# Grouping the products of probabilities and values of a sink attention by whole query tiles

## The chip, the cores and the metric

The kernel runs on one core of one Trainium2 chip. The metric is the time of one execution on the device in microseconds (us), the median over several runs. The core has TensorE (PE in the profile, with its weight loads listed apart as PEld), VectorE (DVE), ScalarE (ACT), GpSimd (POOL) and SyncE (SP, which issues most transfers).

## The reference

Three layers follow each other, all in f32, with 2 batches of 768 positions. The first is an attention of 8 heads of 64 with a sliding window and sink positions; the change is in it.

```
scores = q @ k.T / 8                                   # per head, 768 x 768
keep   = (pos_k < n_sink) | (0 <= pos_q - pos_k < window)   # n_sink 4, window 128
a      = softmax(where(keep, scores, -1e9))
x      = concat_heads(a @ v)                           # 2 x 768 x 512
```

The second layer is `h = relu(x @ w_in)` (512 to 1024), a convolution over 3 neighbouring positions, `h * sigmoid(conv)` and `@ w_out` (1024 to 512). The third is an attention of four experts with a causal mask, of which each position takes the best two. The weights of the second layer come as 64-bit floats.

## The kernel before

The first layer works on query tiles of 128 positions. A batch has 6 tiles, and a tile has 4 pairs of heads, so a batch has 24 steps: step 4q + p is pair p of query tile q. All the work of a layer is laid out on one axis of steps by `run_phases`: every stage of the work on a pair or a tile has a lag in steps, and at each step the stages run in the order that the string `ORD1` gives. What is emitted first stands first in its engine's queue, and each engine works through its queue in order. Batch 1 starts at step 24 and the second layer at step 30.

For batch 0 the stages that matter are these, with the method, the line by which the profile knows it, and the step at which it runs:

- S, scores (`a1_S`): TensorE multiplies queries by keys of the pair's two heads (L484), at the pair's own step. VectorE adds the mask and takes the row maximum (L486), ScalarE takes the exponential with the row sum (L489). Both are emitted with S. Batch 1 does its scores with smaller multiplications (L471).
- T, transposes (`a1_T`): TensorE transposes the probabilities (L545) one step later, and ScalarE copies them to SBUF (L501, tile `PT`).
- V, values (`a1_V`): TensorE multiplies values by the transposed probabilities (L587) into one PSUM bank that holds the output of the whole query tile (`a1O`). It is taken at a tile's first V and read by `x_norm` at step 4q + 10. The lag of V is `pv`, and the third element of its entry says how many steps are gathered: a group is run as a whole, at the lag counted from its first member.
- r, rT, rB: the reciprocals of the sums (L497) at step 4q + 4, their transpose on TensorE (L514) at 4q + 5, and two transfers to DRAM and back that spread them over partitions (R).
- sT, sL, sV (from the third tile on): the probabilities of the sink positions are transposed (L567) at 4q + 6, split (L574) and multiplied by the sinks' values (L595) into the same bank at 4q + 8.
- xm, xh, xl: the output is scaled by the reciprocals (L529), and split in two parts for the next layer (L501, L617).

Between these, background work turns the 64-bit weights of the second layer into f32: ScalarE takes absolute values (L339), VectorE shifts and merges bits (L343, L346, L349, L413). It is emitted by a credit that each step tops up, so its places in the queues do not depend on V.

The order at one step, of batch 0 alone, is: S, sL, V, rB, sV, xm, rT, sT, T, r, xh. The lines that decide where V runs are these:

```
first = i - i % g[0] if g else i
at.setdefault(o + math.floor(lag + first * rate), []).append((k, m, i, fn))
```

Before, V of pairs 0 and 1 of tile q runs at step 4q + 4, and V of pairs 2 and 3 at step 4q + 6.

Of the kernel before, what the change touches and what calls it, by code (L numbers as in the profile page):

```python
# [70 lines left out]
BG0 = 550  # L71
BG1 = 650
BG2 = 1200
LAGS = ((1, 2, 1, 4, 3, 4, 5, 5, 2, 7, 7, 9, 11), (1, 1, 2, 6, 3, 4, 5, 3, 2, 5, 6, 7, 7))
LAGM = (1, 2, 3)
A2_N = 2
EVT = 'aaadadada'
# [11 lines left out]
class Kernel:  # L89
# [538 lines left out]
    def attn_phase(self, b, start, lags, misc):  # L628

        r, gather, tr, pv, sT, sL, sV, rB, rT, xm, xh, xl, halo = lags  # L630
        steps = [(qt, pr) for qt in range(NT) for pr in range(NPAIR)]

        def each(fn):
            return lambda i: fn(b, *steps[i])

        def last(fn, lo=0):
            def go(i):
                qt, pr = steps[i]
                if pr == NPAIR - 1 and qt >= lo:
                    fn(b, qt)  # L640

            return go

        st = {
            "r": (r, last(self.a1_r)), "rT": (rT, last(self.a1_rT)), "rB": (rB, last(self.a1_rB)),
            "xm": (xm, last(self.x_norm)), "S": (0, each(self.a1_S)), "T": (tr, each(self.a1_T)),
            "V": (pv, each(self.a1_V), 4 if b else 2), "gather": (gather, each(self.a1_gather)), "sT": (sT, last(self.a1_sinkT, 2)),
            "sL": (sL, last(self.a1_sinkL, 2)), "sV": (sV, last(self.a1_sinkV, 2)), "xh": (xh, last(self.x_hi)),
            "xl": (xl, last(self.x_lo)), "halo": (halo, last(self.x_halo)), "misc": (0, misc[0]), "more": (0, misc[1])}
        return lambda names: (start, len(steps), [st[n] for n in names.split()], RATE1 if b else 1)  # L650
# [466 lines left out]
    def program(self, general):  # L1117
# [5 lines left out]
        with ExitStack() as ctx:  # L1123
# [34 lines left out]
            else:  # L1158
# [18 lines left out]
                self.fixed()  # L1177
                first = [self.attn_phase(b, b * NSTEP, LAGS[b], self.attn_misc(b)) for b in range(B)]
                m1 = NSTEP + MLP_START
# [109 lines left out]
```

## Time and profile before

| | |
|---|---|
| median of 3 runs | 371.52 us (371.45 to 371.52) |
| profiled execution, its time | 371.99 us |
| its span, first to last instruction | 370.1 us |
| around the span | 1.89 us |
| mean granted TensorE clock | 0.996 |

The profile is of one execution. The busy time of an engine is the union of its instructions' spans. Matmuls overlap, and their ends are modelled, so that PE's busy share is not its share of peak. f32 matmuls stand as two records each in the trace, so 16 records of L587 are the 8 products of two pairs of heads. In the chain of waits, a piece lasts until the next piece of the chain can begin, so its times are what one operation adds to the chain. In the timeline, brackets give the idle time of an engine before an instruction, and what ended it.

### The profile page before, as it was taken

Reading aid. Unit: us, or ns where it says so; the run is one execution under the profiler, and the core shown is the slowest. Engines: PE = TensorE matmul, PEld = TensorE weight load, DVE = VectorE, ACT = ScalarE, POOL = GpSimd, SP = SyncE. Lnnn points to the kernel's source line nnn. Section 1 sums busy time; section 2 is a strip of 40 time slices with the busy share of each in tenths; the row PEclk is TensorE's granted clock in tenths of the full one; section 3 lists DMA queues with packets and bytes.
Section 4 is the critical chain, followed back from the end, with each engine's and each line's share of the span. In section 5 each row is a group of like instructions: output and inputs, shape, how many; then the busy total and the mean of one; then the engine's idle time right before and its main releaser. Section 6 shows DMA issues by size and latency. Waiting matters only on the chain.

```text
span 370.1 us, 8877 instructions
## 1 busy us (share of the span) xinstructions
PE 359.7 (97%) x3166; PEld 331.7 (90%) x3166; DVE 273.1 (74%) x850; ACT 261.2 (71%) x746; POOL 118.8 (32%) x230
## 2 busy tenths in 40 slices
PE   8999999899999999999999999999999999999994
PEld 5687877899899999999999999999999899978983
DVE  5689899999887997878756766238668688578731
ACT  4999998766886766546746766249878687849841
POOL 7014120444432342844421322500034144406310
PEclk9999999999999999999999999999999999999998
DMA  7943865353342311000211010000000010101112
GB/s 178 362 140 126 241 220 173 116 186 129 103 128 69 105 30 31 6 25 25 63 44 45 1 58 3 0 2 0 2 3 1 17 42 22 40 0 58 58 51 75
DMA packets 20404, 27.53 MB, mean 74 GB/s; under 512 B 2080, under 2 KB 12928, under 8 KB 20352
## 3 DMA queue, kind: packets, MB, share of 16 engines
q1 hardware_dynamic: 19120, 26.22, 22.2%
q10 hardware_dynamic: 1232, 0.66, 0.9%
q8 instruction: 27, 0.44, 0.5%
q14 instruction: 25, 0.20, 0.2%
HBM read 23.68 MB, written 3.19 MB: 73 GB/s over the span
## 4 chain that ended last, share of the span: by engine, by line
PE 77%; DVE 12%; ACT 5%; issue 2%; POOL 2%; DMA 1%; SPq 0%; ACTq 0%; DVEq 0%
PE psB L797 15%; PE psB L753 14%; PE psB L947 9%; PE psB L1061 5%; PE psB L1037 5%; PE psB L875 5%; PE psB L1085 4%; PE psB L587 4%; PE psB L484 4%; PE psB L545 3%; DVE P L486 3%; PE psB L1008 3%; PE psB L1007 3%; PE psB L471 2%; ACT P L489 2%
## 5 line engine op out<-in xcount | busy, mean ns | idle before, releaser
L797 PE MATMUL psB<-g,wouthf 128*128 128x256 f32 x384 | 70.5, 281 | 0.2 <-POOL g L782 0.2
L797 PEld LDWEIGHTS psB<-g,wouthf 128*128 128x128 f32 x384 | 58.9, 188 | 0.6 <-POOL g L782 0.4
L753 PE MATMUL psB<-xh,winhf 128*128 128x258 f32 x192 | 56.5, 294 | 0.0
L1025 POOL TENSOR_SCALAR P<-P,r 128x256 f32<-128x256 f32 (+5 forms) x48 | 30.3, 644 | 79.4 <-DVE r L1023 32.6
L753 PE MATMUL psB<-xh,winlf 128*128 128x258 f32 x192 | 54.3, 283 | 0.0
L753 PE MATMUL psB<-xl,winhf 128*128 128x258 f32 x192 | 54.2, 282 | 0.0
L797 PE MATMUL psB<-g,woutlf 128*128 128x256 f32 x192 | 53.8, 280 | 0.0
L489 ACT ACTIVATE P<-P,nm 128x260 f32<-128x260 f32 (+2 forms) x96 | 46.5, 486 | 10.1 <-DVE nm L486 9.9
L782 POOL TENSOR_TENSOR g<-ht,g 128x256 fp32r<-128x256 f32 x48 | 33.2, 691 | 52.4 <-ACT g L776 46.9
L1014 ACT ACTIVATE P<-P,nm 128x256 f32<-128x256 f32 (+5 forms) x48 | 32.1, 669 | 13.5 <-DVE nm L1013 7.8
L769 ACT ACTIVATE ht<-ht 128x256 f32<-128x256 f32 x48 | 20.1, 418 | 28.3 <-DVE ht L767 28.2
L774 DVE SCALAR_TENSOR_TENSOR ht<-ht 128x256 f32<-128x256 f32 x48 | 24.2, 505 | 18.8 <-ACT ht L769 18.8
L753 PEld LDWEIGHTS psB<-xh,winhf 128*128 128x128 f32 x192 | 36.4, 189 | 0.3 <-ACT ht L756 0.2
L753 PEld LDWEIGHTS psB<-xl,winhf 128*128 128x128 f32 x192 | 36.5, 190 | 0.0
L753 PEld LDWEIGHTS psB<-xh,winlf 128*128 128x128 f32 x192 | 36.2, 189 | 0.0
L797 PEld LDWEIGHTS psB<-g,woutlf 128*128 128x128 f32 x192 | 36.2, 189 | 0.0
L1010 DVE CUSTOM_DVE_ANT_0 P<-psB,causal 128x384 f32<-128x384 f32 (+3 forms) x64 | 30.3, 503 | 5.7 <-PE psB L1008 5.2
L760 POOL TENSOR_SCALAR ht<-ht,cw 128x256 f32<-128x256 f32 x24 | 15.1, 627 | 59.8 <-ACT ht L756 52.3
L767 DVE SCALAR_TENSOR_TENSOR ht<-ht,cw 128x256 f32<-128x256 f32 x48 | 28.3, 589 | 1.7
L545 PE MATMUL psB<-ident,P 128*128 128x128 f32 x176 | 29.0, 281 | 0.2
L947 PE MATMUL psB<-yh,wqh 128*128 128x256 f32 x96 | 27.2, 283 | 0.0
L947 PE MATMUL psB<-yl,wqh 128*128 128x256 f32 x96 | 27.0, 281 | 0.0
(172 smaller groups left out, 961.3 us busy)
## 6 DMA issues: line engine op xcount, KB each, us to landing
raw<-in_w_in_dram SPq DMA_DIRECT2D x8, 512.0 KB, 4.1
raw<-in_w_out_dram SPq DMA_DIRECT2D x8, 512.0 KB, 3.3
v<-in_v_dram SPq DMA_DIRECT2D x12, 256.0 KB, 4.4
R<-rD SPq DMA_DIRECT2D x24, 128.0 KB, 2.9
out_dram<-ot SPq DMA_DIRECT2D x11, 256.0 KB, 2.0
k<-in_k_dram SPq DMA_DIRECT2D x7, 260.0 KB, 3.6
raw<-in_wqkv_dram SPq DMA_DIRECT2D x8, 193.0 KB, 3.0
q<-in_q_dram SPq DMA_DIRECT2D x6, 256.0 KB, 4.5
```

The lines of the kernel that those rows point to most:

```text
L489: nc.scalar.activation(Pt[:, j, :N], Pt[:, j, :N], AF.Exp, bias=nmx[:, j : j + 1], scale=-1.0, accum_out=sums[:, j : j + 1])
L545: nc.tensor.transpose(ps[:, j, c, :], Pt[:, j, c0 : c0 + P], self.ident)
L753: nc.tensor.matmul(ps[:, :XW], w[:, f, kc, :], x[:, kc, :], start=(i == 0), stop=(i == len(ops) - 1))
L767: nc.vector.scalar_tensor_tensor(t1, h[:, 2 : 2 + CH], self.cw[:, 2 * NF + f : 2 * NF + f + 1], t1, op0=ALU.mult, op1=ALU.add)
L769: nc.scalar.activation(t1, t1, AF.Tanh)
L774: nc.vector.scalar_tensor_tensor(t1, t1, 1.0, h[:, 1 : 1 + CH], op0=ALU.add, op1=ALU.mult)
L782: eng.tensor_tensor(g[:, 1], t1, g[:, 0].bitcast(F32), op=ALU.subtract)
L797: nc.tensor.matmul(self.m1y[d // 2][:, d % 2, :], w[:, f, d, :], g[:, k], start=(first and i == 0 and d % 2 == 0), stop=(last and i == 2), ...
L947: nc.tensor.matmul(ps, w[:, kc, c0 : c0 + P], y[:, kc, :], start=(i == 0), stop=(i == len(ops) - 1))
L1010: nc.vector.tensor_tensor_reduce(out=Pt[:, lo:hi], in0=ps[:, : hi - lo], in1=mask, scale=-1.0, scalar=BIG, op0=ALU.add, op1=ALU.min, accum ...
L1014: nc.scalar.activation(Pt[:, :N], Pt[:, :N], AF.Exp, bias=nm[:, 0:1], scale=-1.0, accum_out=sums[:, j : j + 1])
L1025: nc.gpsimd.tensor_scalar(Ps[j][:, :N], Ps[j][:, :N], r[:, j : j + 1], 1.0, op0=ALU.mult, op1=ALU.mult)
```

## The change

V of batch 0 has lag 5 instead of 4, and groups of four steps instead of two, which batch 1 has already. So V of all four pairs of tile q runs at step 4q + 5: pairs 0 and 1 one step later than before, pairs 2 and 3 one step earlier. The bank of the tile's output is taken one step later. Nothing else in the order of emission changes.

```
-LAGS = ((1, 2, 1, 4, 3, 4, 5, 5, 2, 7, 7, 9, 11), (1, 1, 2, 6, 3, 4, 5, 3, 2, 5, 6, 7, 7))
+LAGS = ((1, 2, 1, 5, 3, 4, 5, 5, 2, 7, 7, 9, 11), (1, 1, 2, 6, 3, 4, 5, 3, 2, 5, 6, 7, 7))
...
-            "V": (pv, each(self.a1_V), 4 if b else 2), "gather": (gather, each(self.a1_gather)), "sT": (sT, last(self.a1_sinkT, 2)),
+            "V": (pv, each(self.a1_V), 4), "gather": (gather, each(self.a1_gather)), "sT": (sT, last(self.a1_sinkT, 2)),
```

## Rows read from the trace of the kernel before

**Rows 1.** Page, busy time and share of the span
```profile
PE 359.7 (97%) x3166; PEld 331.7 (90%) x3166; DVE 273.1 (74%) x850; ACT 261.2 (71%) x746; POOL 118.8 (32%) x230
```

**Rows 2.** Windows: length, busy time of each engine, granted clock, DMA
```profile
14.00:28.80 14.80, 14.80 (x121) 11.51 (x120) 11.78 (x44) 14.27 (x47) 2.31 (x8) 1.00 0.67 204
28.80:36.80 8.00, 7.74 (x66) 5.99 (x64) 7.49 (x22) 7.61 (x26) 2.93 (x9) 1.00 0.35 110
36.80:52.70 15.90, 15.86 (x140) 12.73 (x140) 14.72 (x56) 15.21 (x52) 3.84 (x17) 1.00 0.75 232
52.70:95.80 43.10, 40.76 (x394) 36.04 (x394) 39.94 (x113) 32.80 (x105) 14.00 (x27) 1.00 0.44 144
95.80:370.10 274.30, 268.69 (x2384) 257.18 (x2384) 191.20 (x575) 182.94 (x489) 88.58 (x149) 0.99 0.12 37
```

**Rows 3.** Chain of waits from 10 to 60: start, us, what
```profile
18.01 1.02 PE psB L587 x16
...
42.32 1.02 PE psB L587 x16
43.34 0.59 PE psB L595 x4
...
44.40 0.88 PE psB L484 x4
45.28 0.11 PE psB L514
45.39 0.44 PE psB L545 x4
45.82 0.88 PE psB L484 x4
...
47.73 0.26 PE psB L567
...
52.24 0.47 PE psB L471 x4
```

**Rows 4.** Chain of waits of the whole span, a V of batch 1
```profile
117.69 1.90 PE psB L587 x32
```

**Rows 5.** Timeline of DVE, 20 to 60: start, us, instruction, idle before
```profile
21.52 0.43 DVE L486 CUSTOM_DVE_ANT_0 P<-psB,m0x 128x260 f32<-128x260 f32 x1 [0.16 <-PE psB L484]
...
30.57 0.41 DVE L486 CUSTOM_DVE_ANT_0 P<-psB,m1x 128x260 f32<-128x260 f32 x1
...
38.11 0.43 DVE L486 CUSTOM_DVE_ANT_0 P<-psB,m0x 128x260 f32<-128x260 f32 x1
...
44.98 0.43 DVE L486 CUSTOM_DVE_ANT_0 P<-psB,m1x 128x260 f32<-128x260 f32 x1 [0.72 <-PE psB L484]
...
45.79 0.43 DVE L343 TENSOR_SCALAR f64u<-f64u 128x512 int32<-128x512 int32 x1
...
46.30 0.43 DVE L486 CUSTOM_DVE_ANT_0 P<-psB,m1x 128x260 f32<-128x260 f32 x1
...
53.90 0.29 DVE L486 CUSTOM_DVE_ANT_0 P<-psB,m 128x128 f32<-128x128 f32 x1
```

**Rows 6.** Timeline of ACT, 20 to 60, second exponentials of steps 11, 15, 19, 23
```profile
25.44 0.50 ACT L489 ACTIVATE P<-P,nm 128x260 f32<-128x260 f32 x1
...
34.26 0.50 ACT L489 ACTIVATE P<-P,nm 128x260 f32<-128x260 f32 x1
...
41.81 0.49 ACT L489 ACTIVATE P<-P,nm 128x260 f32<-128x260 f32 x1
...
50.44 0.50 ACT L489 ACTIVATE P<-P,nm 128x260 f32<-128x260 f32 x1
```

**Rows 7.** Timeline of all engines, 10 to 25, a weight load of step 8
```profile
17.30 0.30 PEld L484 LDWEIGHTS psB<-k,q 128*128 128x128 f32 x2 [0.31 <-DMA q<-in_q_dram]
```

**Rows 8.** Waits, 14 to 56: who waited for whom, us, times, longest
```profile
DVE P L486 <- PE psB L484: 3.5, 7, 0.7
```

## The prediction

> **What bounds the kernel now.** I read the page first: TensorE is busy 97% of the span, VectorE 74%, ScalarE 71% [rows 1]. That is a mean over stages, so I cut the span by what the chain of waits runs through. The change acts from about 10 to 58 us, where batch 0's steps 4 to 27 run. The windows [rows 2] show three engines close to full there. From 36.8 to 52.7 PE is busy 15.86 of 15.90 us, ACT 15.21 and DVE 14.72. The granted clock is 1.00 throughout, so the clock plays no part. The chain of waits goes through PE from 14 to 28.8 and from 36.8 to 52.7, through ACT and DVE between those and from 52.7 to 95.8 us, where DVE is busy 39.94 of 43.10. After 95.8 it is on PE, busy 268.69 of 274.30. So what delays VectorE by 58 us reaches the end: there is hardly any idle time on it until PE takes over, and hardly any on PE after that.
>
> The three engines form a loop. S(t) feeds the row maximum (DVE), that feeds the exponentials (ACT), and those T(t), which stands behind S(t+1) in PE's queue. PE can therefore be about one step ahead, and no more. The reader is to see in the chain [rows 3] how PE's work is dealt out over a tile's four steps: S costs 0.88 us, T 0.44, V of two pairs 1.02, sV 0.59, rT 0.11, sT behind a V 0.26. Before, heavy steps (S, V, T) and light ones (S, T) alternate: S(21) begins at 44.40 and S(22) at 45.82, 1.42 apart. DVE waits for scores now and then, 3.5 us in 7 waits, none over 0.7 [rows 8].
>
> **What the change removes and adds on PE.** The number of instructions stays. A V of four pairs is to be had from batch 1: 32 records take 1.90 us [rows 4], against 2 x 1.02 = 2.04. What follows a V pays more too (sT 0.26 behind a V, rT 0.11 behind S, so 0.15), and that is paid once a tile instead of twice. So PE's own work falls by 0.14 + 0.15 = 0.29 us a tile.
>
> **What it moves.** Step 4q+4 loses its V: S 0.88 and T 0.44 remain, with sV. Step 4q+5 gets all: S 0.88, V 1.90, rT 0.26, T 0.44, together 3.48 us from one S to the next, where 1.42 lay before. In those 3.48 us VectorE gets the scores of one step only. It has two row maxima and a shift to do in that step (44.98 to about 46.2, 1.2 us) [rows 5], beside what it is behind by then. Behind V in PE's queue stand rT, T(4q+4) and S(4q+6), and for those wait the copy of PT on ACT, then the row maxima of step 4q+6, and all the bit work, x_norm and the split that stand behind them in DVE's queue. So the wait goes from PE's slot to VectorE.
>
> How late is the first row maximum of step 4q+6? PE comes to S(4q+5) after T(4q+3), and that waits for the second exponential of step 4q+3, the gate. From the gate: T 0.44, then 3.48, then some 0.5 from the start of an S to its row maximum (44.98 and 46.30 against 44.40 and 45.82) [rows 3, 5]: 4.42 us. A delay of DVE delays the gate of the next tile by as much. So, for each tile, shift = gate + earlier shift + 4.42 - the start before:
>
> Tile 0: its V moves between steps 4, 5 and 6; S(8) waits anyway until 17.30 for the query transfer [rows 7]. Shift 0.
> Tile 1: S(8) ends at 18.01 [rows 3], later than exponential 7, so the gate is there. 18.01 + 4.42 = 22.43 against 21.52 [rows 5]: +0.91.
> Tile 2: gate 25.94 (25.44 + 0.50) [rows 6]; 25.94 + 4.42 = 30.36 against 30.57: DVE was held by other work there, and the step gives 0.21 back.
> Tile 3: gate 34.76; 39.18 against 38.11: +1.07.
> Tile 4: gate 42.30; 46.72 against 46.30: +0.42.
> Tile 5: gate 50.94. Step 25 is batch 1's, with S of 0.47 [rows 3]: 0.44 + 0.47 + 1.90 + 0.26 + 0.44 + 0.5 = 4.01, so 54.95 against 53.90: +1.05.
>
> Sum: 0.91 - 0.21 + 1.07 + 0.42 + 1.05 = 3.24 us. The 0.29 a tile is in it already, since the 3.48 uses 1.90 and one transition. What PE saves at steps 4q+4 and 4q+6 goes into waiting for exponentials.
>
> **What else moves, costed at nothing.** The last pair's PT is now read one step after its transpose instead of two. Its copy on ACT comes after the exponentials of step 4q+4, and V of the first three pairs, some 1.4 of the 1.90 us, covers it; without that cover it would cost up to a copy, about an exponential's 0.5 us [rows 6]. rT comes some 0.8 us later and with it the write of the reciprocals, and SP's queue holds the loads of q, k and v behind that write; the reciprocals' product is five steps later and the loads' readers several steps, and four steps take 8.2 us (38.11 to 46.30) [rows 5], so that hides it, and without the cover 0.8 us a tile would be lost. The output bank is taken a step later, and v tiles are free a step earlier: a gain of nothing to a few tenths, since no wait of PE for a bank is among the longest of that view [rows 8]. The buffers that tiles get from the pools may fall otherwise; neither sign is excluded, and I take 0.5 us each way.
>
> Made against the profiled 371.99 this gives 375.23. The median is 0.47 below that execution, so I say 374.7 us.
>
> **Bounds.** The price of one long V lies between a gain and a loss. Below: PE alone sets the pace and saves 0.29. Above: a tile pays what tile 3 pays, 1.07, five times, 5.4 us. The nearest rows, DVE's own waits for S [rows 5, 8], show that it already runs dry behind a V of half the length (0.72 at 44.98), so I take the value near the upper end.
>
> **Rivals.**
> A, faster: PE stays the bound, and VectorE and ScalarE have a backlog long enough to last through V. PE's saving then counts where the chain is on PE, about four tiles: 4 x 0.29 = 1.2 us, 370.3. For it speaks PE's 15.86 of 15.90 us [rows 2]. Against it: it decides from a backlog of 3.48 - 1.2 - 0.5, about 1.8 us at S(4q+5), and the rows of step 21 show none, as DVE waited 0.72 us there. The Trainium skill, TensorEngine Tiling (Array Packing), Key Properties, says that a change of tiling mode drains TensorE. V loads 64 columns and its neighbours 128, so by that rule halving the changes is a gain; the trace agrees with 0.15 us behind a V, and the sum by that alone would be A's.
> B, the same: the holes in VectorE are taken up by idle time that it had. From 14 to 28.8 it had 3.0 us of it, from 36.8 to 52.7 1.2 us [rows 2]. Tile 2 shows such a case. But the sum above already counts where DVE was late anyway, and holes at fixed places of its queue can't be moved. 371.5. By the Trainium skill, Perfetto Trace Analysis, Identifying the Most-Contended Engine, TensorE is to be judged by its weight loads; those fill 12.73 of 15.90 us against ACT's 15.21 [rows 2], and a change that leaves ACT's work alone would move little.
> C, slower by part: VectorE, once behind, arrives at each S(4q+5) with a backlog of about 1 us, since xl, the reciprocals and bit work pile up at step 4q+4; then only the first hole and half of the others count, 0.9 + 0.5 + 0.2 + 0.3, about 1.9 us, 373.4.
>
> **How the numbers follow.** My forecast, the full sum within a microsecond (373.8 to 376.2), has 0.50. C has 0.25 (372.3 to 373.8), B 0.12, A 0.13. A measurement here tells 0.2%, or 0.75 us, from no change. All of the forecast and C lies beyond it, so slower has 0.75, the same 0.12, faster 0.13. The range leaves out A (0.13) and about 0.06 of the rest: from 371.2, which takes in B, to 376.3, the forecast with the pools' 0.5 and another microsecond.
>
> **What would show it.** In the changed kernel V of batch 0 should stand as 32 records of about 1.9 us. VectorE's waits for S from 14 to 56 us should rise from 3.5 us to about 6, with single ones over 1 us right before the row maxima of steps 10, 18, 22 and 26. These should start near 22.4, 40, 48.5 and 57.1 us. DVE's busy time should not change, and PE's last dense stage should begin some 3 us after 95.8. I am wrong if the waits for S are no longer than before (A), if the row maximum of step 26 comes late but the end does not (B), or if the shift at tile 3 or 5 is under half of what I give (C).

## The result, and the profile after

The changed kernel takes 376.43 us (375.22 to 377.08, 6 runs) against 371.63 us (371.45 to 372.41, 6 runs): a ratio of the means of 1.0119, with a 95% interval of 1.0099 to 1.0139. I had said 374.7 with 371.2 to 376.3, and slower with a chance of 0.75. The direction is as forecast; the median lies 0.1 us above the range. The range was set against a median before of 371.52, so it allows 4.8 us more; the means differ by 4.4 us. The profiled execution took 375.49 us with a span of 373.7, so 3.6 us more than the span before. It is one of the two fastest of the six. The other 1.2 us of the median are not in it; the second half of the experiments looks for them.

The five row maxima that the sum was about, in VectorE's timeline of the changed kernel:

```profile
22.28 0.43 DVE L486 CUSTOM_DVE_ANT_0 P<-psB,m0x 128x260 f32<-128x260 f32 x1 [1.60 <-PE psB L484]
...
31.04 0.41 DVE L486 CUSTOM_DVE_ANT_0 P<-psB,m1x 128x260 f32<-128x260 f32 x1
...
39.82 0.43 DVE L486 CUSTOM_DVE_ANT_0 P<-psB,m0x 128x260 f32<-128x260 f32 x1 [1.25 <-PE psB L484]
...
48.52 0.43 DVE L486 CUSTOM_DVE_ANT_0 P<-psB,m1x 128x260 f32<-128x260 f32 x1 [1.15 <-PE psB L484]
...
57.40 0.29 DVE L486 CUSTOM_DVE_ANT_0 P<-psB,m 128x128 f32<-128x128 f32 x1 [1.39 <-PE psB L471]
```

Four of them now begin right after a wait of 1.15 to 1.60 us for scores, where [rows 5] show at most 0.16 at the same instructions. They stand for steps 10, 14, 18, 22 and 26, and start 0.76, 0.47, 1.71, 2.22 and 3.50 us later than in [rows 5].

The chain of waits of the changed kernel, tile 4's third step (start, us, what):

```profile
44.62 0.88 PE psB L484 x4
45.50 1.90 PE psB L587 x32
47.40 0.20 PE psB L514
47.60 0.44 PE psB L545 x4
48.04 0.45 PE psB L484 x2
48.49 0.02 issue
48.52 0.43 DVE P L486
```

S(21) begins at 44.62 and S(22) at 48.04, 3.42 us apart where 1.42 lay [rows 3]. In between stand V of 1.90, rT and T, and VectorE's row maximum follows the first half of the scores at once.

What became of the delay, in the windows of the changed kernel (columns as in [rows 2]) and in its waits from 14 to 56 us:

```profile
52.70:99.40 46.70, 43.80 (x422) 38.20 (x424) 42.03 (x122) 35.24 (x112) 15.28 (x33) 1.00 0.46 142
99.40:373.70 274.30, 268.48 (x2384) 257.02 (x2384) 190.82 (x575) 182.71 (x489) 88.44 (x149) 1.00 0.12 37
```

```profile
DVE P L486 <- PE psB L484: 5.4, 6, 1.6
...
PE psB L595 <- DVE SPT L574: 2.2, 2, 1.6
```

The last window is cut 3.6 us later than in [rows 2] and holds the same 2384 products, with PE busy 268.48 us against 268.69. In the chains of waits, of the kernel before and of the changed one, the piece that begins the last stage comes 3.5 us later:

```profile
95.77 0.66 PE psB L587 x8
```

```profile
99.28 0.66 PE psB L587 x8
```

So nothing of the 3.50 us of step 26 was taken up on the way. The second of the two waits is one that I had not counted: PE stands still for the sinks' split on VectorE, once for 1.58 us.

### The profile page after: what moved, and what is told of

It reads as the page before. It is cut to its first block, busy times and chain, and to the rows that moved or that the text cites. A ratio compares the mean times of both kernels' runs of the same rounds, so it can differ in the third digit from the quotient of the medians.

```text
span 373.7 us, 8867 instructions
## 1 busy us (share of the span) xinstructions
PE 359.0 (96%) x3166; PEld 331.8 (89%) x3166; DVE 271.9 (73%) x850; ACT 262.1 (70%) x746; POOL 118.3 (32%) x230
## 4 chain that ended last, share of the span: by engine, by line
PE 73%; DVE 14%; ACT 7%; issue 2%; POOL 2%; DMA 1%; ACTq 0%; DVEq 0%
PE psB L797 15%; PE psB L753 14%; PE psB L947 9%; PE psB L1061 5%; PE psB L1037 5%; PE psB L875 5%; PE psB L1085 4%; PE psB L587 4%; ACT P L489 3%; DVE P L486 3%; PE psB L1008 3%; PE psB L1007 3%; PE psB L545 2%; PE psB L484 2%; PE psB L471 2%
```

## The experiments

Theory 1 is the prediction's: the next scores stand behind a long V in TensorE's queue, VectorE runs dry, and the price of each V depends on where the gate and VectorE's other work are. Theory 2: a V of 32 records costs wherever it stands. Theory 3: the cause is the later lag, with the bank and buffers that it holds longer. Each time is compared with runs of the kernel before on the same chip.

**The lag alone** (`lag5_pairs`), from the kernel before:

```
-LAGS = ((1, 2, 1, 4, 3, ...
+LAGS = ((1, 2, 1, 5, 3, ...
```

> Only the lag of V is changed, to 5; the groups stay at two pairs, so V runs at steps 4q+5 and 4q+7. Theory 1 (the next scores stand behind a long V, and VectorE runs dry): from one S to the next lie 2.6 us at most, so row maxima come no later than before except 0.2 us in tile 3; 371.2 to 372.4. Theory 2 (a V of 32 records costs wherever it stands): the same, as there is none. Theory 3 (the later lag, the bank and the pools' buffers cost): most of the loss of 3.6 to 4.8 us is here, 374 or more.

Measured 372.0 us against 372.22 (0.9993, 0.9984 to 1.0002). The lag, the bank and the buffers cost nothing that shows. Theory 3 falls.

**The group at another step** (`lag6_tile`), from the changed kernel:

```
-LAGS = ((1, 2, 1, 5, 3, ...
+LAGS = ((1, 2, 1, 6, 3, ...
```

> As the changed kernel, all four pairs together, but at step 4q+6. Theory 1: what counts is what VectorE has to do at that step. There it has x_norm and two pieces of bit work after its row maxima. By the same sum (gate, now the exponential of step 4q+4, + 4.42) the row maxima of steps 11, 15, 19 and 23 come at 23.5, 32.4, 40.8 and 48.5 against 24.3, 32.5, 40.6 and 49.4 before: no hole over 0.3 us, 371.0 to 372.6. Theory 2: as long as the changed kernel, 375 to 377. Theory 3: a later lag still, so no better than the changed kernel.

Measured 373.26 us against 372.22 (1.0029, 1.0017 to 1.0041), 3.9 us less than the changed kernel on the same chip. The long V is the same, only its place differs, so theory 2 falls as the whole cause. Some of the 3.9 us may be the clock, which is treated below: the four runs of the changed kernel on this chip have a mean granted clock of 0.994 to 0.995, those of lag 6 0.997 to 1.0. Between the two profiles without a fall of the clock in this stretch, the spans differ by 2.1 us (371.6 against 373.7). My figure was still too good. VectorE's waits for scores in its timeline:

```profile
42.05 0.43 DVE L486 CUSTOM_DVE_ANT_0 P<-psB,m0x 128x260 f32<-128x260 f32 x1 [0.71 <-PE psB L484]
...
50.56 0.43 DVE L486 CUSTOM_DVE_ANT_0 P<-psB,m1x 128x260 f32<-128x260 f32 x1 [0.37 <-PE psB L484]
...
57.66 0.29 DVE L486 CUSTOM_DVE_ANT_0 P<-psB,m 128x128 f32<-128x128 f32 x1 [0.47 <-PE psB L471]
```

These are three holes of 0.37 to 0.71 us, where I had said none over 0.3; another of 1.12 us stands at step 7, where 0.68 lay before. A sum of this kind is good to some 0.4 us a tile.

**One pair at a time** (`each_pair`), from the kernel before:

```
-            "V": (pv, each(self.a1_V), 4 if b else 2),
+            "V": (pv, each(self.a1_V), 4 if b else 1),
```

> V of batch 0 at lag 4, one pair at each step, 8 records at a time. Theory 1: the steps are even and VectorE's waits for S fall, but PE pays two more changes a tile of 0.29 us each; where PE sets the pace (tiles 1 and 4) that shows: 372 to 374, with single waits of VectorE for S under 0.7 us. Theory 2: shorter pieces are better, 371.5 or less. Theory 3 (lag and buffers): nothing to say, within 0.5 us of before.

Measured 374.42 us against 372.22 (1.0057, 1.0043 to 1.007), 0.4 above theory 1's range. Shorter pieces are not better, and groups of two lie between two losses. The waits for S, 3.1 us in all against 3.5 [rows 8], hardly fell, and some singles (0.83 before step 10) were over 0.7. VectorE also waited 0.58 us for the load of v before step 21 and 0.88 us for GpSimd before step 22, which I had not counted. What part of the 2.2 us is PE's own work I did not separate, so that the changeovers are the cost is not shown.

**The changed kernel again** (`after_again`).

> The changed kernel once more, for the size of the loss on one chip with the others: 375.2 to 377.1, of which the profile of before and after explains 3.6 us.

Measured 377.16 us (376.59 to 377.79) against 372.22, 1.0125, just above what I had said. Its profiled execution is one of the long ones, with a span of 376.0, and is read below.

**One tile at a time** (`wide_tile2`, `wide_tile3`), from the kernel before. The other tiles keep their pairs at steps 4q+4 and 4q+6.

```
+WIDE = (3,)            # (2,) in wide_tile2
...
+                if b or (qt in WIDE) != skip:
+                    fn(b, qt, pr)
...
+            "V": (pv, tiles(self.a1_V, b == 0), 4 if b else 2), "Vw": (5, tiles(self.a1_V, False), 4),
```

> Only tile 2 of batch 0 has its four pairs together at step 4q+5; the others are as before. Theory 1: VectorE is held by other work at step 14 until 30.6 and the scores come at 30.4, so nothing is lost: 371.6 to 372.6, within 0.2% of before. Theory 2 (a long V costs 0.6 us or more wherever it stands): 372.8 or more.

> Only tile 3 is changed. Theory 1: the row maximum of step 18 comes 1.0 to 1.3 us later than before, VectorE waits about 1.2 us there, and the end moves by as much: 373.0 to 373.7 against 372.2 of before. Theory 2: the same as tile 2 alone. If later stages took the delay up, it would be within 0.3 us of before.

Tile 2 alone: 372.22 against 372.01 (1.0015, 1.0006 to 1.0023), within the 0.2%. Tile 3 alone: 372.88 (1.0029, 1.0018 to 1.004), so 0.9 us, where I had said 0.8 to 1.5. From the timelines of VectorE, tile 2's kernel first, then tile 3's (their lines are one further on than those of before):

```profile
30.65 0.41 DVE L487 CUSTOM_DVE_ANT_0 P<-psB,m1x 128x260 f32<-128x260 f32 x1
```

```profile
39.35 0.43 DVE L487 CUSTOM_DVE_ANT_0 P<-psB,m0x 128x260 f32<-128x260 f32 x1 [1.25 <-PE psB L485]
...
46.80 0.43 DVE L487 CUSTOM_DVE_ANT_0 P<-psB,m1x 128x260 f32<-128x260 f32 x1
...
54.40 0.28 DVE L487 CUSTOM_DVE_ANT_0 P<-psB,m 128x128 f32<-128x128 f32 x1
```

With tile 2 alone, step 14 starts at 30.65 against 30.57 [rows 5]: in the profile the same change costs nothing there, and the median moves by 0.2 us. What holds VectorE in front of step 14 is a shift (L343) that waits for ScalarE and then takes 1.46 us, where another takes 0.43 [rows 5]. The kernel before, then the changed kernel:

```profile
29.18 1.46 DVE L343 TENSOR_SCALAR f64u<-f64u 128x512 int32<-128x512 int32 x1 [0.49 <-ACT f64u L339]
```

```profile
29.67 1.45 DVE L343 TENSOR_SCALAR f64u<-f64u 128x512 int32<-128x512 int32 x1 [1.10 <-ACT f64u L339]
```

So the long V is not free there because VectorE has work in store: it waits 1.10 us in the changed kernel too, only for ScalarE. With tile 3 alone, step 18 is 1.24 us late after a wait of 1.25. By step 22 only 0.50 of it is left, since there VectorE had waited 0.72 for scores before [rows 5] and no longer does; and 0.50 arrives at step 26 and at PE's last stage (96.26 against 95.77); I have no rows for the other 0.4 of the 0.9 us. So a hole is partly paid from the next idle time, if the next tile leaves it any; in the changed kernel each next tile opens a hole of its own.

**Transposes a step later** (`t2_lag6_tile`), from the changed kernel:

```
-LAGS = ((1, 2, 1, 5, 3, ...
+LAGS = ((1, 2, 2, 6, 3, ...
```

> Transposes of batch 0 one step later (lag 2) and all four pairs together at step 4q+6. Theory 1: the scores no longer stand behind a transpose that waits for the exponential just before, so TensorE can be two steps ahead and VectorE has a backlog when the long V comes: holes smaller than with lag 6 alone, 371.0 to 372.6. Theory 2: as long as any long V, over 373. If buffers run out (probabilities live a step longer): waits of TensorE or VectorE for other engines, over 373.

Measured 373.55 us (1.0039, 1.0026 to 1.0052), no better than lag 6 alone (1.0029): a miss. Its waits from 14 to 62 us suggest why TensorE did not run further ahead:

```profile
DVE P L486 <- PE psB L484: 2.9, 4, 1.3
...
PE psB L514 <- DVE su L497: 1.6, 3, 1.0
PE psB L514 <- ACT P L489: 1.2, 3, 0.7
```

In front of the scores now stands rT, which waits for the row sums (on ScalarE) and reciprocals (on VectorE) of the step just before. By this reading the gate moved to another instruction and stayed as near. It is argued and not tried: with lag 6 alone, rT waits 2.1 us for the reciprocals as well, though not for ScalarE.

**Work for the hole** (`after_xm6`), from the changed kernel; `x_norm` one step earlier, and the transfers to it:

```
-LAGS = ((1, 2, 1, 5, 3, 4, 5, 5, 2, 7, ...
+LAGS = ((1, 2, 1, 5, 3, 4, 5, 4, 2, 6, ...
```

> The changed kernel, with the scaling of a tile's output (x_norm, 0.6 us on VectorE) one step earlier, at 4q+9, and its transfers too; TensorE's order stays. This puts work of VectorE between the row maxima of the next tile's second and third step, where the hole is. Theory 1: the waits for S right before the third step of tiles 2 to 5 get about 0.6 us shorter, nothing else waits longer, and the end comes 1.5 to 2.4 us sooner: 374.0 to 375.2 where the changed kernel takes 376.4 to 377.2. If TensorE's own work or the later T and copies set the pace, the time stays. If the transfers of the reciprocals are not there in time, it gets longer.

Measured 374.42 us (374.16 to 374.59) against 376.07 of the changed kernel on the same chip, 1.65 less, and 1.0067 (1.0054 to 1.0081) of before. TensorE's order is the same in both. From the timeline of VectorE:

```profile
22.00 0.69 DVE L529 TENSOR_TENSOR R<-psB,R 128x512 f32<-128x512 f32 x1 [1.69 <-DMA R<-rD]
...
45.98 0.69 DVE L529 TENSOR_TENSOR R<-psB,R 128x512 f32<-128x512 f32 x1
46.58 0.42 DVE L343 TENSOR_SCALAR f64u<-f64u 128x512 int32<-128x512 int32 x1
...
47.99 0.43 DVE L486 CUSTOM_DVE_ANT_0 P<-psB,m1x 128x260 f32<-128x260 f32 x1 [0.99 <-PE psB L484]
...
56.64 0.29 DVE L486 CUSTOM_DVE_ANT_0 P<-psB,m 128x128 f32<-128x128 f32 x1 [1.15 <-PE psB L471]
```

`x_norm` (L529) now stands in the hole of step 21, and the row maxima of steps 22 and 26 come at 47.99 and 56.64 instead of 48.52 and 57.40. The waits are only 0.16 to 0.29 shorter, not 0.6 as I had said. The work that left the steps after the hole lets the gate of the next tile come sooner, so most of the gain shows in where the next scores start. The first hole did not shrink: in place of the 1.60 us for scores, VectorE now waits 1.69 us for the transfer of the reciprocals in front of the first `x_norm`. Some of the 1.65 us may again be the clock, since the runs here have a mean of 0.997 to 1.0 and four of the five of the changed kernel 0.991 to 0.995; between the two profiles without a fall in this stretch, the spans differ by 1.2 us (372.5 against 373.7). With TensorE's order unchanged, work moved into VectorE's idle time gave this back, which supports that this idle time is what the change costs.

**The transposes in front of half the V** (`split_around_T`), from the changed kernel: pairs 2 and 3 behind T in the order of step 4q+5.

```
-... a0.sT a0.T a0.misc ...
+... a0.sT a0.T a0.V2 a0.misc ...
```

> All four pairs still at step 4q+5, but pairs 2 and 3 behind the transposes of that step, so that rT, T and the copies behind them come 0.9 us sooner and the next scores come no sooner. Theory 1: the scores are what is late, so the holes stay, and a third piece of V costs one more change of 0.3 us a tile: 376.0 to 378.0. If the late transposes and copies were the cause: 374 or less.

Measured 378.53 us (376.94 to 379.2) against 376.07 on the same chip (1.0176 of before, 1.0152 to 1.0201). The transposes and copies came sooner and the time got longer. In the timeline of VectorE the holes stay, each 0.15 to 0.35 us longer than in the changed kernel:

```profile
22.82 0.43 DVE L486 CUSTOM_DVE_ANT_0 P<-psB,m0x 128x260 f32<-128x260 f32 x1 [1.90 <-PE psB L484]
...
40.92 0.43 DVE L486 CUSTOM_DVE_ANT_0 P<-psB,m0x 128x260 f32<-128x260 f32 x1 [1.51 <-PE psB L484]
...
49.95 0.43 DVE L486 CUSTOM_DVE_ANT_0 P<-psB,m1x 128x260 f32<-128x260 f32 x1 [1.50 <-PE psB L484]
...
59.13 0.29 DVE L486 CUSTOM_DVE_ANT_0 P<-psB,m 128x128 f32<-128x128 f32 x1 [1.54 <-PE psB L471]
```

So it is the scores that are late, not the transposes. The loss of 2.5 us is more than I had said; the longer holes are 1.1 of it, and the row maximum of step 26 is 1.73 late. I have no rows for the rest.

**The clock.** In the first six runs of the changed kernel two have a mean granted clock of 0.999 and 1.0 and take 375.49 and 375.22 us; the four with 0.995 take 376.25 to 377.08. This is a hint and no more, because the mean also counts time in which TensorE has nothing to do: the 0.996 of the kernel before comes from the end of its span, behind TensorE's work (columns as in [rows 2]):

```profile
365.00:370.00 5.00, 0.10 (x1) 0.00 (x0) 0.22 (x1) 0.37 (x1) 0.00 (x0) 0.71 0.34 116
```

In the profile of `after_again`, windows of one microsecond (the last three columns are granted clock, DMA share, GB/s), then PE's timeline and VectorE's row maximum of step 26, and then two lines of PE's timeline in the profile of the changed kernel without a fall:

```profile
52.00:53.00 1.00, 0.00 (x0) 0.00 (x0) 0.97 (x6) 0.35 (x1) 0.00 (x0) 1.00 0.62 223
53.00:54.00 1.00, 0.65 (x6) 0.66 (x7) 0.97 (x2) 1.00 (x5) 0.19 (x1) 1.00 0.93 247
54.00:55.00 1.00, 1.00 (x9) 0.70 (x7) 0.97 (x6) 0.84 (x4) 0.94 (x6) 0.73 0.65 217
55.00:56.00 1.00, 1.00 (x10) 0.91 (x10) 0.97 (x8) 1.00 (x5) 0.21 (x1) 0.50 0.02 6
56.00:57.00 1.00, 1.00 (x13) 1.00 (x12) 0.58 (x2) 1.00 (x5) 0.00 (x0) 0.50 0.80 221
57.00:58.00 1.00, 1.00 (x14) 1.00 (x12) 0.00 (x0) 0.16 (x2) 0.00 (x0) 0.56 0.83 328
58.00:59.00 1.00, 1.00 (x15) 0.66 (x11) 0.00 (x0) 0.34 (x2) 0.00 (x0) 1.00 0.00 0
```

```profile
53.35 0.66 PE L595 MATMUL psB<-SPT,vsr 128*128 128x128 f32 x4 [1.58 <-DVE SPT L574]
53.84 0.62 PE L545 MATMUL psB<-ident,P 128*128 128x128 f32 x4
54.40 0.77 PE L471 MATMUL psB<-k,q 64*128 64x128 f32 x4
55.10 3.31 PE L587 MATMUL psB<-PT,v 128*64 128x128 f32 x32
```

```profile
59.28 0.29 DVE L486 CUSTOM_DVE_ANT_0 P<-psB,m 128x128 f32<-128x128 f32 x1 [2.70 <-PE psB L471]
```

```profile
52.78 0.66 PE L595 MATMUL psB<-SPT,vsr 128*128 128x128 f32 x4 [1.58 <-DVE SPT L574]
...
54.26 2.27 PE L587 MATMUL psB<-PT,v 128*64 128x128 f32 x32
```

PE stands still for 1.58 us in front of the sinks' product of tile 4, since the split of the sinks (L574) is late on VectorE. About a microsecond after it works again the granted clock falls from 1.00 to 0.50, from 2.4 to 1.2 GHz, for some 3 us, and V of tile 5 takes 3.31 us instead of 2.27 in the profile of the changed kernel without a fall. VectorE's wait behind it (step 26) is 2.70 instead of 1.39: 1.3 us more, at a place where every delay reaches the end. The Trainium skill, TensorE: Matmul & The Clock Gate, HAM oscillation — how this bites in real kernels, describes it: waits that leave TensorE idle let its clock gate close again, and the work behind them runs at half the clock. The rows of this execution agree in the fall behind an idle time. They do not agree in its length: the page's waits, for transfers, are each longer than the 1.58 us here. The profile that stood behind the result has the same gap of 1.58 us and no fall, and so has that of `split_around_T`, whose clock is 1.00 from 40 to 100 us. So the gap does not always bring one.

To try it, the gap was filled (`after_filled`, twice, the second time beside the changed kernel, `after_third`):

```
+        if (b, qt) == (0, 4):
+            self.spin(14)
```

> The changed kernel, with 14 products of zeros (1.5 us at full clock) put in front of the sinks' product of tile 4, where TensorE stood still for 1.58 us before a fall of the granted clock. They add work whose result nobody reads. If that gap brings the fall: no fall in the profile, every run near the two of the changed kernel that had none, 375.0 to 376.0, about 1.2 us below its median. If the fall has another cause (chance, the long V itself): 376.4 to 377.4 and a clock of 0.995 as before. VectorE's holes stay either way, so the time stays over 374.5.

> The changed kernel with the gap in front of tile 4's sinks filled, beside the changed kernel on one chip: 1.0 to 1.4 us less than it, if the fall of the clock behind the gap is what the gap costs; the same, if not.

> The changed kernel beside the other three on one chip: 376.4 to 377.4, with a clock of 0.995 in most runs.

Measured 375.76 us (1.0104, 1.009 to 1.0119) the first time, three of four runs within the 375.0 to 376.0. On one chip, 375.85 us (375.3 to 376.75) with the gap filled against 376.07 (375.5 to 377.31) without: 0.2 us, not the 1.0 to 1.4 that I had expected; the 376.07 is itself 0.3 below what I had said. In both profiles with the gap filled the clock is 1.00 from 52 to 60 us. But in the second, and in that of `after_third`, it falls a tile later. First a window and a line of PE's timeline of the second `after_filled`, then the same two of `after_third`:

```profile
62.00:63.00 1.00, 1.00 (x8) 0.80 (x8) 0.97 (x7) 0.69 (x3) 0.00 (x0) 0.50 0.67 194
```

```profile
61.09 0.74 PE L597 MATMUL psB<-SPT,vsr 128*128 128x128 f32 x4 [0.88 <-DVE SPT L574]
```

```profile
63.00:64.00 1.00, 1.00 (x5) 1.00 (x6) 0.38 (x2) 0.84 (x3) 0.00 (x0) 0.50 0.05 18
```

```profile
60.62 0.66 PE L595 MATMUL psB<-SPT,vsr 128*128 128x128 f32 x4 [0.87 <-DVE SPT L574]
```

Each of the three falls in this stretch came within 3 us of such a wait of PE for the sinks' split. But of the four profiles with the gap of 1.58 us (`split_around_T` among them) one has a fall right behind it, and of the six with one of 0.87 or 0.88 us two. Filling the first gap did not end the falls and did not change the time, so that the gap is the cause is not shown, and what decides whether a fall comes stays open. As to the price, the spans with and without a fall differ by 0.6 us (`after_third` against the profile behind the result) and by 0.9 (the two of `after_filled`); in `after_again` the wait behind V is 1.3 us longer.

`after_again` is slow from its start too. Its first scores, products of 128x128 (L484), take a median of 421 ns, against 275 in the profile behind the result; 421 ns is also the median of V's products in the stretch at 0.50, against 273 without a fall. The windows give a granted clock of 1.00 at the start, so the mean does not show this. The row maximum of step 10 comes 0.57 us later than in the profile behind the result, and that of step 22 still 0.56.

## Why the prediction was right, and what it left out

The working went from one gate to the next, and can be compared tile by tile. The shift that each tile adds at its third row maximum, forecast and measured (differences of the five starts above and [rows 5]):

| tile | forecast, us | measured, us |
|---|---|---|
| 1 | +0.91 | +0.76 |
| 2 | -0.21 | -0.29 |
| 3 | +1.07 | +1.24 |
| 4 | +0.42 | +0.51 |
| 5 | +1.05 | +1.28 |
| sum | 3.24 | 3.50 |

V of four pairs: forecast 1.90 us, measured 1.90 in tile 4's chain. From S(21) to S(22): forecast 3.48, measured 3.42, since rT behind V took 0.20 where I had 0.26. That the delay reaches the end: the last stage begins 3.5 us later and holds the same work. DVE's waits for scores from 14 to 56 us: forecast some 6, measured 5.4, and 1.39 behind tile 5's V.

Rival A, PE as the bound, fails on the same rows: the 0.14 us that V saves on PE are there, but go into waits. Behind V the rows show 0.09 us more for rT and 0.15 for sT; no run shows whether V and its neighbours differ in tiling mode. Rival B, idle time that takes the delay up, holds for tile 2, where the idle time is a wait for ScalarE, and for 0.74 of the 1.24 us of tile 3's hole when that stands alone. Rival C, the holes getting smaller once VectorE is behind, does not show: tiles 3 to 5 cost more than the forecast, not less. Of what was costed at nothing, the pools, the bank and the lag cost nothing (`lag5_pairs`). The cover of the copy of PT was short in tile 5, where V took 2.27 us with a wait of 0.3 for PT.

So the mechanism, the places and the sizes of the holes came out as worked out. What the working left out starts at the sentence "The granted clock is 1.00 throughout, so the clock plays no part". It read the clock of the kernel before, in which PE has hardly a gap in this stretch. But a VectorE that is late is late for TensorE too: I followed its delay to the row maxima, and not to the split of the sinks, for which PE then waits 1.58 us at a stretch. In two of the three profiles of the changed kernel the clock falls within 3 us of such a wait. The four of the first six runs with the lower mean clock average 376.66 us, the two others 375.36. Falls of the clock and slow starts are large enough for these 1.3 us, but the runs do not separate them. Over all 15 runs of the changed kernel the three with a mean clock of 0.999 or 1.0 are the fastest (375.22 to 375.50 us); with the gap filled the order does not hold (0.994 with 375.30, 1.0 with 375.88). That the clock is what lifts the median 0.1 us over the range is therefore likely, and not shown.

None of the kernels tried beats the one before; groups of two, at lag 4 or 5, stay best.

## What to carry to other kernels

Where three engines hand work round in a loop and all are near full, how the feeding engine's work is dealt out counts as much as its sum: merging two pieces saved TensorE some 0.2 us a tile (0.14 in V and 0.09 behind it) and took up to 1.3 us a tile from VectorE. To price such a move, take the event that gates the feeder, add the feeder's queue up to the next thing that the other engine wants, and compare it with what that engine still has to do; the same change was free in one tile, behind a wait for a third engine, and 1.2 us in the next. Then follow the delay back to the feeder: TensorE stood idle as well, and in some executions its clock fell soon after.

## What was not expected of the hardware

The granted clock fell to 0.50 about a microsecond after a gap of 1.58 us in one execution, with gaps of 0.87 and 0.88 us nearest in two others, and did not fall behind the same 1.58 us gap in three (`after`, `after_third`, `split_around_T`). TensorE's first scores take 275 ns in some executions and 421 in others, while the granted clock reads 1.00 in both; the wait for the first keys is shorter in the slower one (0.54 us in `after_again`, 0.88 in the profile behind the result). A shift of 128x512 on VectorE that takes 0.43 us elsewhere took 1.46 in the kernel before and 1.45 in the changed one, each time while GpSimd ran a product of 32x512 for 1.3 us; whether that is the cause was not tried.
